# First batch: the sums of four values as products with a matrix of ones and zeros, taken from local windows that are loaded at the beginning

## The chip, the cores and the metric

The kernel runs on one core of a Trainium2 chip. The metric is device microseconds of that core for one execution. The core has TensorE (PE, with its weight loads shown as PEld), VectorE (DVE), ScalarE (ACT), GpSimd (POOL), and SyncE (SP), whose queue issues every DMA of this kernel. Each engine works through its own instructions in a fixed order; semaphores make one engine wait for another or for a DMA.

## The reference, cut to what matters

Attention for 4 batches of 8 heads, 576 positions of 64 numbers; each output is a coarse attention over means of four positions plus a local attention over a band of plus or minus three positions. Then a softplus MLP, then a mixture of experts with one expert per token.

```python
q_d = q.reshape(B, H, Sd, factor, D).mean(axis=3)      # factor = 4, Sd = 144
k_d = k.reshape(B, H, Sd, factor, D).mean(axis=3)
v_d = v.reshape(B, H, Sd, factor, D).mean(axis=3)      # the sums of four values
out_up = np.repeat(sm_attn(q_d, k_d, v_d), factor, axis=2)
mask = np.abs(pos[:, None] - pos[None, :]) < factor
scores = np.where(mask, scale * np.matmul(q, k.transpose(0, 1, 3, 2)), -1e9)
out_local = np.matmul(softmax(scores), v)
...
x = softplus(x @ w_in) @ w_out                         # 2304 x 512, 512 x 2048 x 512
out = gate * relu(x @ w1[e]) @ w2[e]
```

## The kernel before

Attention is cut into jobs. For each batch there are four `Down` jobs (one for each pair of heads, `hp`), which do the coarse attention, and twelve `Local` jobs (three thirds `j` of the positions, four pairs of heads). A job has six steps (`st_T`, `st_S`, `st_E`, `st_N`, `st_Ta`, `st_PV`): transposes, scores, exponentials, normalisation, transposes of the weights, products with the values. The steps of successive jobs are interleaved with lags of 0, 2, 3, 4, 6 and 7, and a scheduler puts the instructions of each engine into their final order.

**The head.** Before the MLP begins, the jobs of batch 0 run alone as far as its first 384 tokens need. In this part the first weights of the MLP are converted as well: `w_in` and `w_out` come as 64-bit floats, each chunk of 512 KB is loaded into a tile with the tag `raw` and turned into 32-bit floats by `from_f64`, one ACT instruction (L439) and four DVE instructions (L440 to L443). There are 32 chunks: four are converted in the head, the rest in the first block of the MLP (block 0), between its products `ph` (L579) and `py` (L619, L622) and the attention of batch 1.

**Tiles.** The tag `raw` has six buffers. They hold the weight chunks, the values `vr` of each `Down` job, and from batch 1 on its queries and keys `qr`, `kr`. For batch 0, `qr` and `kr` take other tags. The `Local` jobs read windows of 70 positions of the values: a tile `lv` (three buffers) holds three windows for four heads and is filled by three DMAs (L291). All these loads stand in SP's one queue, in program order as the scheduler leaves it, so that a load which waits for a free buffer holds back all loads behind it.

**The sums of four values.** A `Down` job loads its values as 72 partitions with rows of four positions (`vr`, L144), and `pre` adds them up: for batch 0 in one DVE reduction (L160), for later batches in three POOL additions (L155, L158). The result `vs` is an operand of `st_PV` (L248).

**Clock.** `warm` puts extra products with the identity matrix (L264) between the attention's products of the head.

In the tables and rows, `pT` and `pA` are transposes, `pS` scores, `pO` products with values, `dmx` the row maxima of a `Down` job, `de` its exponentials, `ls` those of a `Local` job, `laT` and `daT` the transposed weights, `xN` and `xf` the attention's output, `cva` the working tile of a conversion. A TensorE product of 32-bit floats leaves two records in the trace, so "x6" of them are three products.

Of the kernel before, what the change touches and what calls it, by code (L numbers as in the profile page):

```python
# [9 lines left out]
F32 = mybir.dt.float32  # L10
# [4 lines left out]
ALU = mybir.AluOpType  # L15
# [3 lines left out]
B, H, S, D = 4, 8, 576, 64  # L19
NT, DM, DFF = 2304, 512, 2048  # L20
E, FE = 8, 1024
FACTOR = 4
SD = S // FACTOR
SDH = SD // 2
# [5 lines left out]
TH = 192  # L30
NTH = S // TH
QB = 64
QD = SD // 3
KW = QB + 6
# [8 lines left out]
NC1 = DFF // 128  # L43
# [12 lines left out]
def band_attention__softplus_mlp__top1_moe(  # L56
# [14 lines left out]
    nc = tc.nc  # L71
# [49 lines left out]
    class Down:  # L121
# [3 lines left out]
        def load(self):  # L125
            b, h0 = self.b, 2 * self.hp
            self.raw = []
            for src, nm in ((q, "qr"), (k, "kr")):
                tag = {"qr": "wis", "kr": "wos"}[nm] if b == 0 else "raw"
                on_pe = b < PE_TRANSPOSED  # L130
                t = mlp.tile([RP, RT, 2, D] if on_pe else [128, NBLK, 32], F32, tag=tag, name=nm,
                             bufs=RAWB if tag == "raw" else 2)
                for h in range(2):
                    if on_pe:
                        nc.sync.dma_start(out=t[:, :, h, :], in_=src[b, h0 + h].rearrange("(p r) d -> p r d", r=RT))
                        continue
                    for c in range(2):
                        p0 = h * D + c * 32
                        nc.sync.dma_start(
                            out=t[p0:p0 + 32],  # L140
                            in_=src[b, h0 + h, :, c * 32:(c + 1) * 32].rearrange("(n t) d -> t n d", t=32))
                self.raw.append(t)
            t = mlp.tile([SDH, 2, 2, FACTOR, D], F32, tag="raw", name="vr", bufs=RAWB)
            nc.sync.dma_start(  # L144
                out=t.rearrange("p h a r d -> p (h a) (r d)"),
                in_=v[b, h0:h0 + 2].rearrange("h (a p r) d -> p (h a) (r d)", a=2, p=SDH, r=FACTOR),
            )
            self.raw.append(t)

        def pre(self):  # L150
            self.vs = apool.tile([SDH, 2, 2, D], F32, tag="vs", name="vs", bufs=4)
            x = self.raw[2].rearrange("p h a r d -> p (h a) r d")
            o = self.vs.rearrange("p a h d -> p h a d")
            if 4 <= self.b * NPAIR + self.hp < 16:
                G.tensor_tensor(out=x[:, :, 0:2], in0=x[:, :, 0:2], in1=x[:, :, 2:4], op=ALU.add)  # L155
                for h in range(2):
                    hs = slice(2 * h, 2 * h + 2)
                    G.tensor_tensor(out=o[:, h], in0=x[:, hs, 0], in1=x[:, hs, 1], op=ALU.add)  # L158
            else:
                V.tensor_reduce(out=o, in_=self.raw[2].rearrange("p h a r d -> p h a d r"), axis=AX.X, op=ALU.add)  # L160
# [65 lines left out]
                             accum_out=self.den[:, i, :])  # L226

        def st_N(self):
            den = self.den[:, :, 0]
            V.tensor_scalar(den, den, 1e-9, float(FACTOR), ALU.add, ALU.mult)  # L230
            V.reciprocal(den, den)
            (G if self.b * NPAIR + self.hp >= 4 else V).tensor_tensor(out=self.at, in0=self.at, in1=self.den.to_broadcast([2 * QD, 3, SD]), op=ALU.mult)
# [22 lines left out]
    qkT, vw = {}, {}  # L255
# [10 lines left out]
    def pa(name):  # L266

        if not started[0]:
            nps[0] += 1
            if nps[0] % 2:  # L270
                return psy.tile([128, 512], F32, tag="py", name=name)
        return psa.tile([128, 512], F32, tag="pa", name=name)
# [3 lines left out]
    def pairs(n):  # L276
# [2 lines left out]
            return [(h, i) for i in range(n) for h in range(2)]  # L279
        return [(h, i) for h in range(2) for i in range(n)]  # L280

    class Local:
        def __init__(self, b, j, hp):
            self.b, self.j, self.hp = b, j, hp
            self.w0 = [min(max(TH * j + QB * i - 3, 0), S - KW) for i in range(3)]

        def load_v(self):
            hs = slice(2 * self.hp, 2 * self.hp + 4)
            t = apool.tile([KW, 3, 4, D], F32, tag="lv", name="lv", bufs=3)
            for i in range(3):  # L290
                nc.sync.dma_start(  # L291
                    out=t[:, i], in_=v[self.b, hs, self.w0[i]:self.w0[i] + KW, :].rearrange("h p d -> p h d"))
            vw[self.b, self.j, self.hp // 2] = t

        def pre(self):
            pass
# [91 lines left out]
    def load_after(n):  # L388

        while loads and loads[0][0] <= n:  # L390
            loads.pop(0)[1]()
# [28 lines left out]
    def make_mask():  # L420
        G.memset(mask, 0.0)
        for hh in range(2):
            for sl, lo in ((slice(0, 1), -3), (slice(1, 4), 0), (slice(4, 5), 3)):
                m = mask[hh * QB:(hh + 1) * QB, sl, :]
                n = sl.stop - sl.start
                for sgn, base in ((1, -lo), (-1, lo + 6)):
                    G.affine_select(
                        out=m, in_=m, compare_op=ALU.is_ge, fill=MASKED, base=base,
                        pattern=[[0, n], [sgn, KW]], channel_multiplier=-sgn,
                    )  # L430
# [376 lines left out]
    if 0:  # L807
        ps = pa("pW")
        for i in range(0):
            T.matmul(ps[:, :128], ident, ident, start=True, stop=True)  # L810
    jobs[0].pre()
    make_mask()
    load_after(-1)
    for st in range(12 + LAG):
        attn_to(pre_end[st])
# [213 lines left out]
```

## Time and profile before

| | |
|---|---|
| median of 3 runs | 798.44 us (793.97 to 799.4) |
| the profiled execution | 798.25 us, its span 796.2 us |
| busy, share of the span | PE 95%, DVE 69%, POOL 59%, ACT 57% |
| granted TensorE clock, mean over the span | 0.977 |

The profiled execution's own time is 2.05 us more than its span. A busy PE is not PE at its peak, since products are pipelined and their ends are modelled. Shares over the whole span hide that the program has three parts with different limits: the head up to some 64 us, block 0 up to some 156 us, and the rest.

### The profile page before, as it was taken

To read this page: it belongs to the slowest core of one execution; us is meant where nothing else is said; L and a number is where in the kernel's file an instruction comes from. 1 tells how busy PE (TensorE), PEld (TensorE's weight loads), DVE (VectorE), ACT (ScalarE), POOL (GpSimd) and SP (SyncE) were. 2 spreads that over 40 slices of the span, in tenths; PEclk is the share of its full clock that TensorE was granted. 3 is DMA by queue.
4 is the path that set the end of the run, shared out by engine and by line. 5 is a ranking of instruction groups with operands and counts; after the bars stand their busy time and mean duration, and the time that the engine had idled before them with its cause. 6 is when DMAs were issued, how large, how long until landed. Compare 5 with 4: busy or idle time off the path is not lost.

```text
span 796.2 us, 13871 instructions
## 1 busy us (share of the span) xinstructions
PE 752.5 (95%) x4917; PEld 658.4 (83%) x4918; DVE 551.7 (69%) x1103; ACT 451.8 (57%) x1164; POOL 472.6 (59%) x451
## 2 busy tenths in 40 slices
PE   5886998899999999999999999999989999999994
PEld 4664655579799989899999999999977889899893
DVE  6979999967885787988654675556996385275221
ACT  5835566656566646666565656475646265355332
POOL 3435623757776666867566666666689366455541
PEclk9866999999999999999999999999999999999998
DMA  8849666415100251301000100080102022002002
GB/s 195 189 92 274 186 209 178 83 23 116 26 12 16 64 88 31 68 22 51 2 12 12 52 2 1 1 331 1 40 1 79 21 61 80 0 1 80 1 0 84
DMA packets 111448, 55.46 MB, mean 70 GB/s; under 512 B 89594, under 2 KB 102412, under 8 KB 111372
## 3 DMA queue, kind: packets, MB, share of 16 engines
q1 hardware_dynamic: 111371, 54.50, 25.7%
q8 instruction: 41, 0.67, 0.4%
q14 instruction: 36, 0.29, 0.1%
HBM read 45.05 MB, written 9.44 MB: 68 GB/s over the span
## 4 chain that ended last, share of the span: by engine, by line
PE 69%; DVE 17%; issue 4%; ACT 3%; DMA 3%; POOL 2%; SPq 1%; DVEq 0%; POOLq 0%; ACTq 0%
PE py L622 18%; PE ph L582 18%; PE py L913 12%; PE ph L764 9%; PE pO L344 2%; PE pS L311 2%; DVE cva L442 2%; PE ph L579 2%; PE pA L336 2%; DVE cva L440 1%; DVE g L604 1%; PE pS L210 1%; DVE cva L441 1%; DVE g L605 1%; DMA vr<-in_v_dram 1%
## 5 line engine op out<-in xcount | busy, mean ns | idle before, releaser
L622 PE MATMUL py<-g,wos 128*128 128x384 f32 x1056 | 209.8, 341 | 7.2 <-ACT wos L478 4.0
L622 PEld LDWEIGHTS py<-g,wos 128*128 128x128 f32 x1056 | 181.9, 188 | 14.1 <-ACT wos L478 5.2
L582 PE MATMUL ph<-xT,wis 128*128 128x384 f32 x960 | 184.3, 339 | 0.4 <-POOL wis L479 0.4
L582 PEld LDWEIGHTS ph<-xT,wis 128*128 128x128 f32 x960 | 166.3, 188 | 2.7 <-POOL wis L479 1.0
L479 POOL TENSOR_TENSOR wos<-wo,wos 128x512 fp32r<-128x512 f32 x88 | 124.0, 1410 | 40.5 <-ACT wos L478 37.3
L479 POOL TENSOR_TENSOR wis<-wi,wis 128x512 fp32r<-128x512 f32 x80 | 107.1, 1340 | 53.0 <-ACT wis L478 46.4
L588 ACT ACTIVATE ga<-ph 128x384 f32<-128x384 f32 x96 | 46.7, 486 | 72.3 <-PE ph L582 62.6
L603 DVE SCALAR_TENSOR_TENSOR ga<-ph,ga 128x384 f32<-128x384 f32 x88 | 48.4, 550 | 47.5 <-ACT ga L590 47.2
L769 DVE TENSOR_TENSOR u<-ph,u 128x384 f32<-128x384 f32 x60 | 33.2, 555 | 60.3 <-PE ph L764 60.1
L764 PE MATMUL ph<-xs,ws 128*128 128x384 f32 x378 | 73.6, 337 | 1.3 <-DVE u L769 0.9
L325 ACT ACTIVATE ls<-ls,lst 128x70 f32<-128x70 f32 x144 | 49.3, 344 | 43.9 <-DVE lst L319 38.6
L478 ACT CAST wos<-wo 128x512 fp32r<-128x512 f32 x88 | 54.2, 617 | 33.7 <-PE py L622 32.3
L764 PEld LDWEIGHTS ph<-xs,ws 128*128 128x128 f32 x378 | 67.0, 188 | 5.1 <-DVE u L769 1.3
L605 DVE TENSOR_TENSOR g<-ga,g 128x384 fp32r<-128x384 f32 x80 | 69.5, 868 | 1.6
L913 PE MATMUL py<-wos,gs 128*128 128x512 f32 x270 | 68.2, 394 | 0.3 <-ACT gs L773 0.3
L331 POOL TENSOR_TENSOR ls<-ls,lst 128x210 f32<-128x210 f32 x48 | 31.4, 656 | 54.7 <-DVE lst L330 36.8
L604 DVE CAST g<-ga 128x384 fp32r<-128x384 f32 x80 | 58.4, 730 | 4.5 <-PE py L622 0.9
L913 PEld LDWEIGHTS py<-wos,gs 128*128 128x128 f32 x270 | 50.1, 188 | 10.0 <-issue 0.6
L590 ACT ACTIVATE ga<-ga 128x384 f32<-128x384 f32 x96 | 50.3, 524 | 2.0
L589 ACT ACTIVATE ga<-ga 128x384 f32<-128x384 f32 x96 | 50.4, 525 | 0.5
L479 POOL TENSOR_TENSOR wos<-w2s,wos 128x512 fp32r<-128x512 f32 x24 | 33.2, 1388 | 27.5 <-ACT wos L478 27.5
L478 ACT CAST wis<-wi 128x512 fp32r<-128x512 f32 x80 | 48.9, 611 | 0.4 <-PE ph L582 0.4
(163 smaller groups left out, 1293.4 us busy)
## 6 DMA issues: line engine op xcount, KB each, us to landing
raw<-in_moe_w_in_dram SPq DMA_DIRECT2D x16, 512.0 KB
raw<-in_moe_w_out_dram SPq DMA_DIRECT2D x16, 512.0 KB
lv<-in_v_dram SPq DMA_DIRECT2D x72, 70.0 KB
vr<-in_v_dram SPq DMA_DIRECT2D x16, 288.0 KB
ydram<-y SPq DMA_DIRECT2D x12, 384.0 KB
yb<-ydram SPq DMA_DIRECT2D x12, 384.0 KB
out_dram<-ob SPq DMA_DIRECT2D x18, 256.0 KB
qr<-in_q_dram SPq DMA_DIRECT2D x48, 72.0 KB
```

Of the source, the lines that this page charges most:

```text
L325: A.activation(s[:, i, :], s[:, i, :], AF.Exp, bias=st[:, 0, i], accum_out=st[:, 1, i])
L478: A.copy(w[:, 0], src)
L479: G.tensor_tensor(out=w[:, 1], in0=src, in1=w[:, 0].bitcast(F32), op=ALU.subtract)
L582: T.matmul(ps[:, :TB], wt[:, w, cc, :], xT[n][:, x, cc, :], start=(i == 0), stop=(i == 3 * CC - 1))
L589: A.activation(a, a, AF.Exp, scale=-1.0)
L590: A.activation(a, a, AF.Ln, bias=1.0)
L603: V.scalar_tensor_tensor(a, ps[:, :TB], 0.0, a, ALU.max, ALU.add)
L604: (A.copy if n < 1 else V.tensor_copy)(g[:, 0, :], a)
L605: (G if n < 1 else V).tensor_tensor(out=g[:, 1, :], in0=a, in1=g[:, 0, :].bitcast(F32), op=ALU.subtract)
L622: T.matmul(yps[n][dc][:, :TB], w[:, a, dsl], g[:, b, :], start=(c == 0 and i == 0), stop=(c == NC1 - 1 and i == 2))
L764: T.matmul(ps[:, :TB], ops[:, w, a, cc, :], xop[p, x][:, l, cc, :], start=i == 0, stop=i == 5)
L913: T.matmul(yps[n][t], g[:, a, t * 128:(t + 1) * 128], w[:, b, :], start=first and c == q and i == 0, stop=last and c == q + NQ and i == 2)
```

## The change

For batch 0 the loads of `vr` and the DVE reductions are gone. All six window tiles of batch 0 are loaded by the `load` of the second and the fourth `Down` job, nine DMAs each, into parts of the tile `wo` that the converted `w_out` needs only later, and not into `lv`. In `st_N` of the first and the third `Down` job, `sums` computes `vs` for two pairs of heads: ten TensorE products of 70 x 72 (the matrix `sel`) by 70 x 256 (a window of four heads), accumulated in a PSUM bank `pV`, then one copy by ACT and one by DVE. `make_sel` builds the matrix on POOL with two memsets and six `affine_select`, in a part of the tile `wi` that is not yet in use. Batches 1 to 3 keep `vr` and `pre`.

```diff
@@ Down.load
+            if b == 0:
+                if self.hp % 2:
+                    for j in range(NTH):
+                        load_window(b, j, self.hp // 2, early[j * 2 + self.hp // 2])
+                return
             t = mlp.tile([SDH, 2, 2, FACTOR, D], F32, tag="raw", name="vr", bufs=RAWB)
...
+        def sums(self):
+            g = self.hp // 2
+            ps = pa("pV")
+            for a in range(2):
+                for i, w in enumerate(range(4 * a, 4 * a + 5)):
+                    x0 = 72 - (16 * w - SDH * a)
+                    o = 0 if w == 0 else 2 if w == 3 * NTH - 1 else 1
+                    T.matmul(ps[:SDH, a * 256:(a + 1) * 256], sel[:, o, x0:x0 + SDH],
+                             early[(w // 3) * 2 + g][:, w % 3, :, :].rearrange("p h d -> p (h d)"), start=i == 0, stop=i == 4)
+            for h in range(2):
+                t = jobs[2 * (self.hp + h)].vs = apool.tile([SDH, 2, 2, D], F32, tag="vs", name="vs", bufs=4)
+                (V.tensor_copy if h else A.copy)(
+                    t, ps[:SDH, :].rearrange("p (a h d) -> p a h d", a=2, h=4)[:, :, 2 * h:2 * h + 2, :])
+
         def pre(self):
+            if self.b == 0:
+                return
...
         def st_N(self):
+            if self.b == 0 and self.hp % 2 == 0:
+                self.sums()
...
+    early = [wo[:KW, 4 + 2 * i:6 + 2 * i, :].rearrange("p c f -> p (c f)")[:, :3 * 4 * D].rearrange(
+        "p (i h d) -> p i h d", i=3, h=4) for i in range(2 * NTH)]
+    sel = wi[:KW, NC1 - 1].rearrange("p c f -> p (c f)")[:, :3 * 152].rearrange("p (o x) -> p o x", o=3)
+
+    def make_sel():
+        G.memset(sel, 0.0)
+        G.memset(sel[:, :, 72:88], 1.0)
+        for o in range(3):
+            m = sel[:, o, 72:88]
+            G.affine_select(out=m, in_=m, compare_op=ALU.is_ge, fill=0.0, base=-3 * o, pattern=[[-FACTOR, 16]],
+                            channel_multiplier=1)
+            G.affine_select(out=m, in_=m, compare_op=ALU.is_ge, fill=0.0, base=FACTOR - 1 + 3 * o, pattern=[[FACTOR, 16]],
+                            channel_multiplier=-1)
+
+    def load_window(b, j, g, t):
+        for i in range(3):
+            w0 = min(max(TH * j + QB * i - 3, 0), S - KW)
+            nc.sync.dma_start(out=t[:, i], in_=v[b, 4 * g:4 * g + 4, w0:w0 + KW, :].rearrange("h p d -> p h d"))
+        vw[b, j, g] = t
...
         def load_v(self):
+            if self.b == 0:
+                return
+            load_window(self.b, self.j, self.hp // 2, apool.tile([KW, 3, 4, D], F32, tag="lv", name="lv", bufs=3))
...
-    jobs[0].pre()
     make_mask()
+    make_sel()
```

Line numbers shift: L172 becomes L193, L210 L231, L239 L262, L248 L271, L264 L287, L291 L322, L311 L351, L336 L376, L344 L384, L456 L496, L460 L500. In the order of instructions, `wo` as an operand in the head is a window of values and `wi` is `sel`.

On PE, early in the head, before: the third set of transposes follows the first local scores.

```order
L210 MATMUL pS<-dkT,dbd_101 96x144 x3
L172 MATMUL pT<-ident,kr 128x96 x6
L311 MATMUL pS<-qkT 64x70 x6
L172 MATMUL pT<-ident,qr 128x96 x6
L210 MATMUL pS<-dkT,dbd_102 96x144 x3
L172 MATMUL pT<-ident,kr 128x96 x6
```

The same place on PE with the change:

```order
L231 MATMUL pS<-dkT,dbd_101 96x144 x3
L193 MATMUL pT<-ident,kr 128x96 x6
L351 MATMUL pS<-qkT 64x70 x6
L162 MATMUL pV<-wo,wi 72x256 x10
L193 MATMUL pT<-ident,qr 128x96 x6
L231 MATMUL pS<-dkT,dbd_102 96x144 x3
L193 MATMUL pT<-ident,kr 128x96 x6
```

The first ten products of the sums now stand between the first local scores and the third set of transposes; all behind them waits for the nine windows that they read.

On PE, in the middle of the head, before: from the transposes of the second `Down` job to the scores of the fourth.

```order
L344 MATMUL pO<-laT,lv 64x64 x6
L264 MATMUL pO<-ident 128x128
L239 MATMUL pA<-ident,de 72x96 x3
L248 MATMUL pO<-daT,vs 64x144
L311 MATMUL pS<-qkT 64x70 x6
L264 MATMUL pS<-ident 128x128
L239 MATMUL pA<-ident,de 72x96 x3
L210 MATMUL pS<-dkT,dbd_102 96x144 x3
```

The same place on PE with the change:

```order
L384 MATMUL pO<-laT,wo 64x64 x6
L287 MATMUL pO<-ident 128x128
L262 MATMUL pA<-ident,de 72x96 x3
L162 MATMUL pV<-wo,wi 72x256 x10
L271 MATMUL pO<-daT,vs 64x144
L351 MATMUL pS<-qkT 64x70
L231 MATMUL pS<-dkT,dbd_102 96x144 x3
```

The second ten stand ahead of the scores of the fourth `Down` job, from which its maxima, exponentials and normalisation follow on DVE and ACT.

On SP, from the third chunk of `w_in` to the second chunk of `w_out` (the first that is converted after the head), before:

```order
L456 DMA raw<-in_moe_w_in_dram 128x4x256
L139 DMA qr<-in_q_dram 32x18x32 x4
L139 DMA kr<-in_k_dram 32x18x32 x4
L144 DMA vr<-in_v_dram 72x4x256
L291 DMA lv<-in_v_dram 70x4x64 x3
L139 DMA qr<-in_q_dram 32x18x32 x4
L139 DMA kr<-in_k_dram 32x18x32 x4
L291 DMA lv<-in_v_dram 70x4x64 x3
L144 DMA vr<-in_v_dram 72x4x256
L460 DMA raw<-in_moe_w_out_dram 128x1024
```

The same place on SP with the change:

```order
L496 DMA raw<-in_moe_w_in_dram 128x4x256
L322 DMA lv<-in_v_dram 70x4x64 x4
L542 DMA wg<-in_moe_w_gate_dram 128x4x8
L139 DMA qr<-in_q_dram 32x18x32 x4
L139 DMA kr<-in_k_dram 32x18x32 x4
L149 DMA vr<-in_v_dram 72x4x256
L543 DMA bias_b<-in_moe_modality_bias_dram 128x16
L139 DMA qr<-in_q_dram 32x18x32 x4
L139 DMA kr<-in_k_dram 32x18x32 x4
L149 DMA vr<-in_v_dram 72x4x256
L500 DMA raw<-in_moe_w_out_dram 128x1024
```

The two window loads among the queries and keys of batch 1, which waited for buffers of `lv`, are gone from there; the windows of batch 1 stand further ahead, where the three buffers are free. Behind block 0 the order of every engine is as before.

## Rows read from the trace of the kernel before

**Rows 1.** The page, span in 40 equal slices: busy tenths, granted clock.

```profile
PE   5886998899999999999999999999989999999994
DVE  6979999967885787988654675556996385275221

```

**Rows 2.** Busy us by stretch: head, block 0, rest; then clock, DMA share, GB/s.

```profile
0.00:64.00 64.00, 46.18 (x417) 37.27 (x418) 48.03 (x107) 35.69 (x130) 26.09 (x53) 0.83 0.74 172
64.00:156.00 92.00, 85.69 (x483) 53.27 (x484) 91.76 (x196) 55.20 (x162) 45.79 (x42) 0.95 0.68 185
156.00:796.00 640.00, 620.64 (x4019) 567.86 (x4017) 411.86 (x802) 360.96 (x873) 400.68 (x358) 1.00 0.15 43
```

**Rows 3.** The same view in the head; columns PE, PEld, DVE, ACT, POOL, clock.

```profile
10.00:22.00 12.00, 9.50 (x80) 7.94 (x80) 10.79 (x22) 9.19 (x33) 3.72 (x7) 1.00 1.01 232
22.00:26.00 4.00, 4.00 (x30) 3.57 (x29) 3.38 (x6) 3.42 (x15) 1.54 (x3) 0.57 1.08 288
...
36.00:40.00 4.00, 1.88 (x20) 1.30 (x17) 4.00 (x7) 0.78 (x2) 4.00 (x4) 0.89 0.85 198
40.00:52.00 12.00, 11.91 (x80) 9.07 (x80) 6.64 (x19) 4.20 (x17) 4.52 (x6) 0.50 0.36 75
...
56.00:66.00 10.00, 3.08 (x47) 2.30 (x44) 8.05 (x21) 4.07 (x17) 3.96 (x6) 0.68 0.95 256
```

**Rows 4.** The chain that ended last, 0 to 20 us: start, duration, what.

```profile
3.56 4.83 DMA vr<-in_v_dram
8.42 1.93 DVE vs L160
...
11.06 1.75 PE pS L210 x6
```

**Rows 5.** Groups of DVE instructions, 0 to 30 us.

```profile
L160 DVE TENSOR_REDUCE vs<-vr 72x256 f32<-72x1024 f32 x4 | 7.7, 1931 | 1.4 <-DMA vr<-in_v_dram 1.4
```

**Rows 6.** Groups of DVE instructions, 40 to 64 us.

```profile
L339 DVE COPY laT<-pA 70x384 f32<-70x384 f32 x3 | 1.6, 544 | 0.0
```

**Rows 7.** Groups of ACT instructions, 0 to 45 us.

```profile
L242 ACT COPY daT<-pA 72x288 f32<-72x288 f32 x8 | 3.1, 400 | 0.0
```

**Rows 8.** Groups of PE instructions, 80 to 126 us (granted clock 1.00).

```profile
L619 PE MATMUL py<-gN,wo 128*128 128x384 f32 x56 | 19.5, 489 | 0.0
...
L210 PE MATMUL pS<-dkT,dbd 128*96 128x144 f32 x18 | 2.7, 289 | 0.0
```

**Rows 9.** SP's queue in order of time, 40 to 60 us.

```profile
43.92 0.41 SPq L144 DMA_DIRECT2D vr<-in_v_dram  x1
49.24 1.27 SPq L291 DMA_DIRECT2D lv<-in_v_dram  x3
...
56.56 1.37 SPq L291 DMA_DIRECT2D lv<-in_v_dram  x3
58.03 0.36 SPq L144 DMA_DIRECT2D vr<-in_v_dram  x1
58.49 0.36 SPq L460 DMA_DIRECT2D raw<-in_moe_w_out_dram  x1
```

**Rows 10.** What SP's queue waited for, 0 to 140 us: total, times, longest.

```profile
SPq L291 <- PE pO L344: 6.6, 2, 4.8
```

**Rows 11.** The chain that ended last, 28 to 50 us.

```profile
38.29 1.66 DVE de L232
...
40.09 1.15 PE pA L239 x6
```

**Rows 12.** DVE in order of time, 58 to 68 us.

```profile
63.68 1.41 DVE L440 TENSOR_SCALAR cva<-cva 128x512 f32<-128x512 f32 x1 [1.95 <-ACT cva L439]
```

**Rows 13.** POOL in order of time, 0 to 14 us.

```profile
1.71 3.47 POOL L427 TENSOR_SCALAR_AFFINE_SELECT mask<-mask 64x70 f32<-64x70 f32 x12
11.77 0.67 POOL L185 TENSOR_TENSOR ds<-qkT 128x288 f32<-128x288 f32 x1 [6.59 <-DVE qkT L177]
```

More of the change, by code (lines that the diff above doesn't have):

```diff
@@ L287, in load_v @@
         def load_v(self):
[L288 to L293, printed above, removed]
+            if self.b == 0:
+                return
+            load_window(self.b, self.j, self.hp // 2, apool.tile([KW, 3, 4, D], F32, tag="lv", name="lv", bufs=3))
         def pre(self):
```

## The prediction

> **What bounds the kernel now.** I read the slices of the page first [rows 1]: PE is at nine tenths or more nearly everywhere except in the first four slices, and DVE is full in the stretch behind them. The table of busy times by stretch makes three parts of it [rows 2]. In the rest (156 to 796 us) PE is busy 620.6 of 640 us; the change touches nothing there. In block 0 (64 to 156 us) DVE is busy 91.8 of 92 us: the conversion of the weights sets the pace. In the head (0 to 64 us) no engine is full: PE 46.2, DVE 48.0, ACT 35.7 of 64 us. All that the change edits lies in the head, so the question is how much earlier or later block 0 can begin. A microsecond there is a microsecond at the end, since DVE in block 0 and PE behind it leave no slack. The second thing to read is the clock: the head as a whole is granted 0.83, and within it 40 to 52 us stands at 0.50, that is 1.2 instead of 2.4 GHz, with PE busy 11.91 of 12 us [rows 3]. Ahead of that stretch PE is busy only 1.88 of 4 us; in the chain, TensorE's next transposes at 40.09 us wait for the DVE normalisation `de` that ends at 39.95 [rows 11].
>
> The sum is made against the profiled execution, 798.25 us, which is 0.2 us under the median of the runs (798.44). Those runs spread from 794.0 to 799.4, and about 1% (8 us) is what a measurement of this kernel can tell from no change.
>
> **What goes.** DVE loses four reductions of 1.93 us, 7.7 us [rows 5]. The first is on the chain: DVE waits for `vr` until 8.42 us and the first scores start only at 11.06 [rows 4]. Without it that wait and 1.93 us go there. But what is late next are the nine windows, which the sums right behind the first scores need. They stand behind eight loads of queries and keys; I expect them to land near 13 us, about when PE reaches the first sums, so I count the 1.9 us at nothing and keep it as a bound on the good side. The other three reductions lie beside work of PE and ACT. SP loses four loads of 288 KB, and nine window loads move ahead, 630 KB; the DMA engines are busy throughout 10 to 22 us at 232 GB/s [rows 3], which makes 1152 KB about 5.0 us and 630 KB about 2.7 us. So the first weight chunks come about 2 us earlier at most; their conversion is placed behind attention steps, so this is worth nothing.
>
> **What comes: twenty products of 256 columns on PE.** No such product is in the trace. In block 0, 56 records of L619, that is 28 products of 384 columns, take 19.5 us, 0.70 us each, or 0.46 for 256 columns; nine products L210 of 144 columns take 2.7 us, 0.30 each, or 0.53 [rows 8]. The twenty cost 9.3 to 10.7 us at the full clock. I take 9.3, since 256 lies in a dense run of ten, like L619. At the half clock it would be twice that.
>
> The first ten (4.6 us) fall into 10 to 22 us, where PE is idle for 2.5 us [rows 3]; that much is absorbed, and 2.1 us is left. The second ten (4.6 us) fall behind 26 us, where PE works without a gap up to the idle time of 36 to 40 us, so they add in full: 6.8 us. There PE is idle for 2.1 us because `de` of the fourth `Down` job comes late out of a DVE queue full of conversions [rows 3, 11]. With PE 6.8 us later, its other products last until `de` is done; the gap closes: **+4.7 us** at the place that is 40 us now.
>
> **Small additions.** Four copies out of PSUM, two on DVE and two on ACT: the nearest rows are 0.54 us on DVE for 384 columns and 0.40 on ACT for 288 [rows 6, 7]. The two on DVE are under a seventh of what it loses; ACT, nearly full between 14 and 36 us, takes 0.8 us more, and I count that inside PE's delay. If that cover is gone it costs 0.8 us. POOL builds `sel` with two memsets and six selects right after the mask: the mask's twelve take 3.47 us, so six about 1.8, and POOL then stands idle for 6.59 us before its first sum at 11.77 [rows 13]; nobody waits. The windows sit in parts of `wo` and `wi` whose conversions come in block 0, long after the last reader: nothing.
>
> **The clock, term three.** If PE has no gap where it now waits from 38 to 40 us, the fall to 0.50 that follows has no occasion. At full speed the 11.9 us of products in 40 to 52 us would be 6.0. The other engines then limit: DVE has 6.64 us of work there [rows 3], so at most 5.4 us can come back. Steps of one job wait for each other across four engines, so I take 4.0: the balance becomes **+0.7 us**. Bounds: 0, if the clock stays as it is, and 6.0, with a further 1.7 us if the half-speed stretch at 22 to 26 us (granted 0.57) goes as well.
>
> **The queue, term four.** Block 0 cannot start its conversions before the second chunk of `w_out` is there. SP issues it at 58.49 us, behind a window load at 56.56 that had waited for a buffer of `lv` and another at 49.24 that had held the queue for 4.8 us [rows 9, 10]. DVE then stands idle for 1.95 us until 63.68 [rows 12]. With the change both window loads are gone from this place. The queries, keys and `vr` ahead of it still wait for `raw` buffers that DVE's transposes of batch 1 free, so the load moves by about the 2 us of window issue and not by more; DVE's idle time goes: **-2.0 us**, bounds 0 and 2.5.
>
> **Sum.** 798.25 + 4.7 - 4.0 - 2.0 = 796.95, so **797.0 us**. With no help from the clock it is 798.25 + 2.7 = 801.0. With both stretches at full speed and the 1.9 us at the start it is 798.25 + 4.7 - 6.0 - 1.7 - 1.9 - 2.0 = 791.3.
>
> **Rivals.**
> The clock stays as it is: 801.0. For it: PE was busy 11.91 of 12 us at 0.50 and was not given back its speed [rows 3], so filling PE is no warrant. Against it: the fall followed the gap that the change closes.
>
> Full speed through the whole head: 791.3. For it: twenty dense products in a part that had only short ones. This is what the Trainium skill would have, in "TensorE: Matmul & The Clock Gate", section "Part 1: The HAM clock gate (the "warmup" mystery)": the throttled state is the default, and sustained activity releases it. The 12 us at 0.50 with PE busy throughout speak against that rule as the page puts it, and the measurement decides; so it has a small chance.
>
> DVE and not PE bounds the head: then PE's products fill gaps, and block 0 begins earlier by what DVE loses, 7.7 less 1.1 for two copies, and by the 2.0 of its idle time: 798.25 - 6.6 - 2.0 = 789.6. For it: DVE has 10.79 of 12 us in 10 to 22. Against it: DVE has only 6.64 of 12 us in 40 to 52, where PE is full [rows 3].
>
> Slower than before: the sums themselves run at half the clock. The mechanism is the wait in front of them: PE stops at the first ten until nine windows have landed, and the row shows a half-speed stretch at 22 to 26 us behind a part with idle time. Each ten then costs 4.6 us more: 805.6 for one, 810.2 for both, with the rest of the clock as it is. It decides if the windows land later than some 15 us, so that PE has a gap like that of 36 to 40 us.
>
> The head's shift doesn't reach the end, because the pace of block 0 hides it: 798.3. Against it: DVE has 0.2 us of slack in 92 us there [rows 2].
>
> **How the numbers follow.** Forecast (797.0, own range 793 to 800) 0.40; clock as it is (801.0) 0.22; no effect at the end (798.3) 0.12; full clock (791.3) 0.10; DVE bounds (789.6) 0.10; sums at half the clock (over 805) 0.06. Faster by over 1% is below 790.5: most of the DVE case and an edge of the full clock, 0.10. Slower by over 1% is above 806.4: the last case, 0.07 with its edge. Within 1%: 0.83. The range leaves out the last case and half of the DVE case: 790 to 803.5.
>
> **What would show it.** The profile of the changed kernel should have 40 records of L162 in two runs of about 4.6 us each. The first run should start near 13 us with little idle time in front; a wait for a DMA there above 1 us makes the price of the start wrong. The reduction of batch 0 is gone from DVE. The clock in the stretch behind 40 us decides between 797 and 801. The second `w_out` chunk should be issued about 2 us earlier against the attention around it, and DVE's wait for ACT in front of that conversion should be gone; if it stays, term four is wrong. If block 0 begins earlier or later and the total does not follow, the reading of block 0 is wrong.

## The result, and the profile after

The changed kernel takes 800.28 us (median of 20 runs, 794.9 to 803.8), the kernel before 795.2 us on the same chip (20 runs, 791.1 to 800.3). The ratio is 1.0057, with an interval from 1.0039 to 1.0075: slower by 4.5 us (5.1 by the medians), where a gain of 1.3 us was forecast. The kernel before was also 3 us faster in these runs than in the profiled execution (798.25 us) that the sum was made against.

The busy times by stretch of the changed kernel answer to [rows 2] and [rows 3]. Columns are PE, PEld, DVE, ACT, POOL, then granted clock, share of the DMA engines, GB/s.

```profile
0.00:64.00 64.00, 53.62 (x460) 40.94 (x461) 40.79 (x102) 35.65 (x128) 28.41 (x62) 0.99 0.72 167
64.00:156.00 92.00, 84.11 (x477) 53.07 (x478) 90.70 (x198) 56.18 (x166) 42.04 (x39) 0.95 0.62 175
156.00:796.00 640.00, 622.56 (x4022) 570.04 (x4020) 406.53 (x803) 361.36 (x873) 401.82 (x358) 0.99 0.15 43
10.00:22.00 12.00, 12.00 (x45) 7.94 (x46) 3.49 (x10) 3.96 (x16) 1.63 (x3) 1.00 0.81 181
...
40.00:52.00 12.00, 11.77 (x140) 9.40 (x140) 11.36 (x29) 8.36 (x36) 6.61 (x8) 1.00 0.53 99
```

In the head PE has 7.4 us more and DVE 7.2 us less to do than before. The clock column rose from 0.83 to 0.99, and 40 to 52 us is at 1.00, where it was at 0.50. But DVE stands idle for 23.2 us of the head (64 less 40.79), before for 16.0 (64 less 48.03): the work that was taken off DVE became idle time. PE's timeline tells where. Columns are start, duration, instruction, and in brackets the idle time in front of it.

```profile
13.37 8.81 PE L162 MATMUL pV<-wo,wi 70*72 70x256 f32 x20
21.97 1.17 PE L193 MATMUL pT<-ident,qr 96*128 96x96 f32 x6
...
33.13 4.48 PE L162 MATMUL pV<-wo,wi 70*72 70x256 f32 x20
```

The same ten products (20 records) take 8.81 us the first time and 4.48 the second: 0.88 and 0.45 us each. The first ten ran at half speed, and so did the transposes behind them (1.17 us for six records; later in the same trace 0.66). The column of the granted clock shows 1.00 there all the same, so at the beginning of these traces the duration of a known product is the better clock. DVE's timeline has the other end of it, and its first conversion of block 0:

```profile
22.70 0.67 DVE L198 COPY qkT<-pT 128x288 f32<-128x288 f32 x1 [6.10 <-PE pT L193]
...
64.67 0.41 DVE L480 TENSOR_SCALAR cva<-cva 128x512 f32<-128x512 f32 x1
```

DVE waits 6.10 us for the transposes behind the first ten. At 64.67 it doesn't wait for ACT any more (1.95 us in [rows 12]), and SP issues the second `w_out` chunk at 56.61, 1.9 us earlier than in [rows 9]:

```profile
56.61 0.35 SPq L500 DMA_DIRECT2D raw<-in_moe_w_out_dram  x1
```

At the front of SP's queue it is the other way round. First the two first chunks of `w_in` before, then nine windows and these two chunks after:

```profile
18.04 0.97 SPq L456 DMA_DIRECT2D raw<-in_moe_w_in_dram  x2
```

```profile
6.35 4.39 SPq L322 DMA_DIRECT2D wo<-in_v_dram  x9
20.62 0.96 SPq L496 DMA_DIRECT2D raw<-in_moe_w_in_dram  x2
```

The chunks go out 2.6 us later. Nine window loads of 70 KB take 4.39 us of SP's time; each of the four `vr` loads of 288 KB that went took 0.58 to 0.91.

The earlier `w_out` chunk isn't worth anything at the end. A line's summary gives the duration (least, median, greatest, ns) and the first and last start. First the 64 products of block 0 (128 records) before, then after:

```profile
L579 PE MATMUL ph<-xN,wi x128: 485/486/847, 69.4 to 175.0; 128*128 128x384 f32 x128
```

```profile
L619 PE MATMUL ph<-xN,wi x128: 485/486/848, 66.9 to 176.5; 128*128 128x384 f32 x128
```

The first starts 2.5 us earlier, the last 1.5 us later. From the last one to the end of the span it is 621.2 us before and 621.3 after, so what this change costs arises ahead of the last product of block 0. (In the twenty profiles of this study that stretch takes 621.2 to 624.7 us; in some of the other kernels up to 3.5 us of the difference lie there.) Ahead of it DVE's conversions run nearly without a gap behind the head (90.70 of 92 us). Their last line, `wo`, in a second execution of the kernel before (before_again, below) and in the changed kernel:

```profile
L443 DVE SCALAR_TENSOR_TENSOR wo<-raw,cva x16: 657/681/1407, 39.7 to 151.1; 128x512 int32<-128x512 int32 x16
```

```profile
L483 DVE SCALAR_TENSOR_TENSOR wo<-raw,cva x16: 650/680/1080, 43.3 to 155.3; 128x512 int32<-128x512 int32 x16
```

The last conversion starts 4.2 us later, and the last product of block 0 4.3 us later (176.5 against 172.2 in before_again), though the first product starts at 66.9 us in both. In this pair what counts is how much of DVE's work is done when the head ends (50.33 us there, 7.7 of it reductions, 40.79 after), not when the first product starts. In the profile that the prediction rests on, the last conversion starts at 154.8 us: two executions of one kernel lie 3.7 us apart here, so a single profile settles no difference of that size.

### The profile page after: what moved, and what is told of

It is laid out like the page before. It is cut to its first block, busy times and chain, and to the rows that moved or that the text cites. A ratio compares the mean times of both kernels' runs of the same rounds, so it can differ in the third digit from the quotient of the medians.

```text
span 797.8 us, 13950 instructions
## 1 busy us (share of the span) xinstructions
PE 760.3 (95%) x4957; PEld 664.0 (83%) x4958; DVE 538.0 (67%) x1101; ACT 453.2 (57%) x1166; POOL 472.3 (59%) x459
## 4 chain that ended last, share of the span: by engine, by line
PE 72%; DVE 17%; ACT 4%; issue 3%; DMA 2%; POOL 1%; SPq 0%; DVEq 0%; ACTq 0%
PE py L662 19%; PE ph L622 17%; PE py L953 12%; PE ph L804 10%; DVE cva L482 2%; PE pO L384 2%; PE pS L351 2%; PE ph L619 2%; PE pA L376 2%; DVE cva L480 1%; DVE g L644 1%; PE pS L231 1%; DVE ga L643 1%; PE pV L162 1%; DVE g L645 1%
## 5 line engine op out<-in xcount | busy, mean ns | idle before, releaser
L409 POOL TENSOR_TENSOR xT<-xf,xT 128x192 fp32r<-128x192 f32 x40 | 31.0, 776 | 34.4 <-DVE xT L408 29.5
```

## The experiments

Theory A: the half speed of the first ten costs the time. Theory B: the amount of work on PE does. Rivals that came up with the first results: the early loads do (C), or the speed that TensorE is granted in the head, which depends on the gaps that each edit opens or closes (D). All ratios are against the kernel before, run beside it on the same chip.

| kernel | what is edited | us | ratio, interval |
|---|---|---|---|
| before_again | nothing | 795.1 | 1.0001, 0.9977 to 1.0026 |
| sums_later | after, first ten later | 799.3 | 1.0057, 1.0029 to 1.0085 |
| warm_after | after, 8 products at the start | 802.2 | 1.0090, 1.0054 to 1.0125 |
| warm_before | before, 8 products at the start | 805.9 | 1.0139, 1.0115 to 1.0164 |
| win_early | before, early loads | 800.8 | 1.0102, 1.0052 to 1.0151 |
| sums_few | after, 4 of 20 products | 798.0 | 1.0039, 1.0010 to 1.0068 |
| sums_none | after, no products | 800.7 | 1.0063, 1.0031 to 1.0095 |
| sums_twice | after, 40 products | 807.6 | 1.0161, 1.0112 to 1.0210 |
| none_late | before, no reductions | 808.6 | 1.0164, 1.0130 to 1.0199 |
| reduce_const | after's loads, DVE reduces | 801.5 | 1.0066, 1.0040 to 1.0092 |
| win_pool | after, loads by POOL | 816.5 | 1.0269, 1.0235 to 1.0302 |
| after_no_fill | after, no fillers | 804.6 | 1.0106, 1.0071 to 1.0141 |
| before_no_fill | before, no fillers | 797.8 | 1.0022, 0.9996 to 1.0048 |
| none_late_fill | none_late, 64 fillers | 795.2 | 0.9988, 0.9969 to 1.0006 |
| before_fill | before, 64 fillers | 802.2 | 1.0079, 1.0050 to 1.0109 |
| after_fill | after, 64 fillers | 809.5 | 1.0206, 1.0157 to 1.0256 |
| later_fill | sums_later, 64 fillers | 818.0 | 1.0295, 1.0255 to 1.0335 |
| none_early_fill | sums_none, 64 fillers | 803.7 | 1.0112, 1.0074 to 1.0150 |

**before_again.** No edit; the kernel before once more.

> The kernel before, unchanged, once more: a second execution of it with a trace, and a measure of what no change looks like. Both theories: ratio 1.000 within 0.003. The profile of before that the prediction rests on took 798.25 us, 3 us over the median of its 20 runs; if the half-speed stretch at 40 to 52 us belongs to that one execution, this trace lacks it, and the term of the prediction that gives 4.0 us back for it counted a loss that the usual execution doesn't have.

Measured 1.0001. Its profile (span 794.3 us) has the half-speed stretch again: 0.52 at 40 to 44 us and 0.50 at 44 to 48. The last product of block 0 starts at 172.2 us, 2.8 us earlier than in the profile of the prediction, so that one profile lay 2 to 3 us above the usual one.

**sums_later.** The first ten products are called one stage later.

```
         def st_N(self):
-            if self.b == 0 and self.hp % 2 == 0:
-                self.sums()
...
         def st_Ta(self):
+            if self.b == 0 and self.hp % 2 == 0:
+                self.sums()
```

> The changed kernel with the sums called in the step st_Ta and not in st_N, so that on TensorE the first ten products stand behind the third set of transposes and two sets of scores. Theory A (the clock): the first ten ran at half speed, 8.8 us where the second ten took 4.5, because TensorE had not yet been given its full speed; later they run at full speed, about 4.5 us, and the time falls by about 4 us, to 796 us, a ratio of 1.001 to before. Theory B (the amount): twenty products in a head that TensorE bounds cost the same wherever they stand; the time stays at 800 us, ratio 1.006.

The products ran as theory A wanted, in PE's timeline:

```profile
17.80 4.54 PE L162 MATMUL pV<-wo,wi 70*72 70x256 f32 x20
22.17 0.66 PE L262 MATMUL pA<-ident,de 96*72 96x96 f32 x6
```

The ten cost 4.54 in place of 8.81 us, and the time is the same as that of the changed kernel (1.0057 both). The windows show where the 4.3 us went:

```profile
28.00:32.00 4.00, 1.66 (x19) 1.32 (x19) 3.91 (x10) 3.94 (x14) 1.41 (x2) 0.85 0.50 86
32.00:36.00 4.00, 4.00 (x26) 3.42 (x25) 2.87 (x7) 2.11 (x9) 2.09 (x2) 0.50 0.85 159
```

PE, earlier by that much, has a gap (1.66 of 4 us), and half speed follows. Theory A falls for the total; that the gap took the 4.3 us back is a reading of these windows, not a test.

**warm_after and warm_before.** Eight products of the identity at the very beginning, to bring the speed sooner.

```
-    if 0:
+    if 1:
         ps = pa("pW")
-        for i in range(0):
+        for i in range(8):
             T.matmul(ps[:, :128], ident, ident, start=True, stop=True)
```

> The changed kernel with eight products of 128 columns with the identity matrix at the very beginning, while TensorE waits for the first loads (nothing reads their result). Theory A: if they raise the clock before the first ten products, those take about 4.5 us and the time falls to about 796 us; if the records show the first ten still at 8.8 us, the test says nothing on the time but that such products do not raise the clock. Theory B: 800 us or up to 2 us more, ratio 1.006 to 1.008.

> The kernel before with the same eight products at the beginning: the control of the run with them in the changed kernel. Both theories: within 2 us of before, ratio 0.998 to 1.003, since the head of before is not bound by its first scores.

Both are misses: slower by 7 and 11 us than the kernel before. In warm_after the first transposes took 0.66 to 0.69 us, full speed; then it was taken back, and the ten products ran at half speed again (8.74 us). Its windows:

```profile
8.00:12.00 4.00, 3.19 (x26) 2.68 (x25) 2.07 (x4) 1.94 (x6) 1.09 (x2) 0.59 0.78 175
12.00:24.00 12.00, 12.00 (x40) 8.29 (x39) 3.56 (x9) 4.40 (x17) 1.13 (x2) 0.50 0.79 180
```

Behind 12 us PE is busy without a gap and stays at 0.50 for 12 us. Why warm_before loses as much as 11 us its profile doesn't settle: that execution took 799.2 us, 7 less than the median of its runs.

**win_early.** The kernel before, with the first batch's windows loaded at the beginning; the reductions and their own loads stay.

```
+            if b == 0 and self.hp % 2:
+                for j in range(NTH):
+                    load_window(b, j, self.hp // 2, early[j * 2 + self.hp // 2])
```

> The kernel before with one part of the change: the first batch's local values are all loaded at the beginning into the unused chunks, while the sums stay reductions on VectorE with their own loads. Kernel before: median 795.2. If the products are what costs (too much TensorE work in the head, or the half speed of the first ten), this one keeps none of the loss: 793 with the queue's term of the prediction (2.0 us), 795 without it. If the loss of the changed kernel comes from the loads at the beginning or from the order that they bring, 798 to 800.

It loses 5.9 us by the medians without any sums on PE (8 by the ratio; one of its six runs took 811.2 us, the others 799.9 to 802.1). Nine more windows, 630 KB, stand at the beginning, and the `vr` loads that the changed kernel drops are still there: the first `w_in` chunk goes out at 26.02 us (18.04 before, 20.62 in the changed kernel), and DVE waits 4.2 us for `vr` (1.4 before). So its loss can be more than what the loads cost in the changed kernel.

**sums_few, sums_none, sums_twice.** The number of products, with the loads and the copies of the changed kernel. sums_few:

```
-                for i, w in enumerate(range(4 * a, 4 * a + 5)):
+                for i, w in enumerate(range(4 * a, 4 * a + 1)):
```

sums_none copies from `ident` in place of `ps` and has no products. sums_twice:

```
-            for a in range(2):
+            for a in (0, 1, 0, 1):
```

> The changed kernel with one product of the five per half, 4 of 20 in all; four fifths of each sum are left out. Changed kernel: median 800.3. Of 13.3 us of products (8.8 and 4.5) 10.6 go. If TensorE's work in the head is the price, microsecond for microsecond, 790; if half of it lies beside other work, 795; if the price is only the half speed of the first ten (7.0 us of their 8.8 go), 793 to 796; if the loss lies in the loads, in the copies of the sums or in the order, 799 to 801.

> The changed kernel without any product: the tiles of the sums are filled by the same two copies each from a constant, so the first batch's coarse values are left out. It tells what taking the reductions off VectorE was worth. If they stood on the path that sets the end, as the prediction says of the first of them (2.5 us) and of the queue behind them (2.0 us), 788 to 791; if their 7.7 us only become idle time of VectorE, 794 to 796, and the products alone then cost 4 to 6; if the loss lies in the loads, 799 to 801.

> The changed kernel with each ten products made twice (the second time over the first): 13 us more of TensorE work in the same two places, of which 9 us at half speed if the first twenty run as the first ten did, 4.5 us at full. If the amount sets the price, microsecond for microsecond, 810 to 814; if a price of 5 us for 13 us of products holds on, 805; if what the first ten cost is hidden by waits behind them, 800 to 802.

0, 4, 20 and 40 products give 800.7, 798.0, 800.3 and 807.6 us. The last twenty cost 7.3 us, the first twenty nothing that the intervals (about 3 us) can tell: theory B as a price by the microsecond falls too. Nor did the reductions' removal give anything, since sums_none has neither reductions nor products and is no faster. Its windows suggest why the products are free:

```profile
12.00:16.00 4.00, 2.40 (x24) 1.84 (x23) 2.21 (x7) 3.96 (x17) 0.00 (x0) 1.00 0.84 189
16.00:20.00 4.00, 4.00 (x34) 3.64 (x35) 2.10 (x6) 2.36 (x7) 1.63 (x3) 0.62 0.88 199
20.00:28.00 8.00, 7.14 (x44) 5.41 (x42) 3.49 (x10) 5.26 (x22) 2.88 (x5) 0.55 0.92 255
28.00:40.00 12.00, 10.51 (x73) 8.44 (x73) 6.18 (x17) 7.96 (x33) 4.45 (x4) 0.61 0.85 160
```

Without them PE has a gap at 12 to 16 us, and 24 us at little over half speed follow; DVE is idle for 24.3 us of the head. In sums_twice the first twenty products took 17.34 us, all at half speed, and the second twenty 8.80.

**none_late, reduce_const.** Loads and reductions one at a time. none_late is the kernel before without the first batch's reductions and `vr` loads; reduce_const is the changed kernel with the reductions back on DVE, over a constant, in place of `sums`. In none_late:

```
         def pre(self):
+            if self.b == 0:
+                return
```

In reduce_const:

```
+                x = ident[:SDH, :D].rearrange("p (o e d) -> p o e d", o=1, e=1).to_broadcast([SDH, 4, FACTOR, D])
+                V.tensor_reduce(out=self.vs.rearrange("p a h d -> p (a h) d"), in_=x.rearrange("p a r d -> p a d r"),
+                                axis=AX.X, op=ALU.add)
```

> The kernel before without the first batch's reductions and without their loads; the sums' tiles are filled from a constant by two copies each, as in sums_none, so the first batch's coarse values are left out. The local values are loaded as in the kernel before. sums_none (800.7) did the same with the early loads. If the early loads cost the 5 us, 788 to 794; if taking 7.7 us off VectorE only turns into idle time and the loads cost nothing, 794 to 797; if the head without the reductions is slower by itself (its order, or a TensorE that idles and then runs at half speed), 799 to 802.

> The changed kernel's loads with the reductions back on VectorE, over a constant of the same size (so the first batch's coarse values are left out, and no load of their own stands in the queue); no products. Kernel before 795. If the early loads cost the 5 us, 799 to 803; if the loads cost nothing and the head without reductions is slower by itself, 793 to 796.

reduce_const loses as much as the changed kernel with the reductions on DVE and nothing on PE (four of 1.21 us here, where those of the kernel before took 1.93). So from before to after in this order the loads cost 5.2 us, and the two other steps nothing: 1.0066, 1.0063 (sums_none), 1.0057 (after). But reduce_const is not a test of the loads alone: its head is granted 0.81 and its block 0 0.91 (before_again 0.87 and 0.94), with 0.50 throughout 44 to 64 us, so theory D's speed is a rival for these 5.2 us. In the other order it doesn't add up: none_late, with the loads left alone, was forecast at 788 to 802 and took 808.6. Its windows:

```profile
16.00:20.00 4.00, 2.09 (x21) 1.90 (x21) 3.12 (x9) 3.83 (x18) 1.91 (x4) 1.00 0.92 270
20.00:28.00 8.00, 7.12 (x40) 5.54 (x40) 6.14 (x14) 6.02 (x19) 3.43 (x6) 0.57 0.82 158
...
40.00:44.00 4.00, 1.66 (x14) 1.55 (x15) 1.94 (x6) 2.66 (x14) 2.73 (x4) 0.67 0.49 79
44.00:64.00 20.00, 20.00 (x129) 14.89 (x127) 5.96 (x18) 5.57 (x24) 1.82 (x4) 0.50 0.19 38
```

Two gaps of PE (2.09 and 1.66 of 4 us busy), half speed behind each, and in the second case 20 us with PE full at 0.50 and DVE busy only 5.96 of 20 us. Here PE at half speed is the bound of the head: SP waits 13.3 us for a product of PE (L356) that frees a buffer of `lv`, and the second `w_out` chunk goes out at 64.20 us.

**win_pool.** The early loads are issued by GpSimd's queue.

```
-            nc.sync.dma_start(
+            (nc.gpsimd if b == 0 else nc.sync).dma_start(
```

> The changed kernel with the 18 early loads issued by GpSimd's queue in place of SyncE's. SyncE's first loads of w_in then go out some 8.8 us earlier (two rows of nine loads of 4.39 us each stand before them). If the early loads cost by their place in SyncE's queue, 795 to 797; if by the bandwidth that they take from the others, 799 to 802; if the loss has nothing to do with the loads, 800 too, and the two are then told apart by none_late.

A miss, and not the test that it was meant to be: the loads stand on POOL between the mask and `sel`, the last three selects of `sel` start at 20.68 us, and PE stands for 7.17 us in front of the first product.

**after_no_fill, before_no_fill.** Both kernels have 20 filler products of the identity (`warm`, read by nobody); here they have none.

```
         if 4 <= nloc[0] < 12:
-            for i in range(1):
+            for i in range(0):
                 T.matmul(ps[:, 384:384 + 128], ident, ident[:, :128], start=True, stop=True)
```

> The changed kernel without its 20 filler products (identity by identity, nobody reads them; 9.26 us of TensorE's time between 31 and 57 us). There TensorE was busy nearly without a gap at full speed. If its work sets the head and the 20 sums alone hold its speed, 793 to 797; if gaps open without the fillers and half speed follows, 800 to 806, with a granted clock well under 0.99 in the first 64 us; if neither matters to the end, 800.

> The kernel before without its 20 filler products (11.3 us of TensorE's time, part of it at half speed). If the speed that is granted in the head sets its length, a lower clock than 0.83 there and 798 to 805; if TensorE's amount of work sets it, 788 to 793; if neither, 795.

Taking 9.3 us of work off a PE that was nearly full made the changed kernel 4.4 us slower. The windows show a gap and half speed behind it:

```profile
40.00:44.00 4.00, 1.62 (x16) 1.38 (x18) 3.97 (x14) 3.26 (x16) 1.93 (x4) 0.65 0.74 118
44.00:64.00 20.00, 17.87 (x158) 13.70 (x155) 17.16 (x43) 9.13 (x41) 9.19 (x15) 0.50 0.67 165
```

But these are not shown to be the cause. DVE did more in this head than in the changed kernel's (44.87 us, 40.79), and its last conversion starts at 153.6 us, not at 155.3. The loss comes later: the last product of block 0 starts at 177.5 us (176.5), and from there to the end it is 624.7 us (621.3). Why is open.

The kernel before loses 1.7 us by the ratio, 3.8 at most by its interval. That the shorter work and the longer half speed (0.50 from 40 to 60 us) about cancel there is a reading that no run tests.

**none_late_fill.** More fillers, from an earlier point on: 64 in place of 20, where the expectation says twice as many.

```
-        if 4 <= nloc[0] < 12:
-            for i in range(1):
+        if 2 <= nloc[0] < 12:
+            for i in range(2):
```

> none_late (808.6; granted clock 0.72 in the first 64 us, at half speed from 44 to 64 us with TensorE busy throughout) with fillers twice as many and from an earlier point on; the first batch's coarse values are left out there too. If the half speed is what made none_late slow and gaps before it are its cause, the clock stays up and the time falls to 794 to 802 in spite of more than 10 us of added products; if the amount of work sets the head, 812 to 820.

With 44 products more, that nobody reads, the kernel is 13.4 us faster than none_late. The same windows as of none_late:

```profile
16.00:20.00 4.00, 4.00 (x46) 3.81 (x45) 2.78 (x7) 3.27 (x15) 1.58 (x3) 1.00 0.97 280
20.00:28.00 8.00, 7.70 (x79) 6.58 (x77) 6.62 (x15) 6.96 (x26) 3.24 (x5) 1.00 0.75 157
...
40.00:44.00 4.00, 4.00 (x47) 3.30 (x46) 1.65 (x6) 1.79 (x8) 2.54 (x3) 1.00 0.53 116
44.00:64.00 20.00, 17.64 (x181) 14.09 (x180) 16.36 (x42) 9.17 (x40) 7.86 (x14) 0.84 0.71 168
```

No gap, no half speed up to 56 us, and SP issues the second `w_out` chunk at 50.91 us, 13.3 us earlier. This is the strongest evidence for D. It is not D alone: the fillers also change the order that the scheduler makes on DVE and SP.

**before_fill, after_fill, later_fill, none_early_fill.** The same edit in four other kernels.

> The kernel before with the fillers of none_late_fill (twice as many, from an earlier point on). If half speed in the head (0.50 at 40 to 48 us) costs it anything that fillers give back, 790 to 794; if the reductions on VectorE are then what it waits for, so that none_late_fill's 795.2 is the better for having none, 797 to 803; if the head's length does not reach the end, 795.

> The changed kernel with the same fillers. It was at full speed from 25 to 62 us already, with TensorE busy nearly all the time, so more fillers are only more work there: 803 to 812 if TensorE's work sets its head; 794 to 799 if half speed was still what cost it.

> sums_later (799.3; first ten products at full speed, then a gap at 29 us and half speed from 30 to 38 us) with the same fillers. If the gap and the half speed took back what the full speed of the first ten had given, 793 to 797; if the products' amount is the cost, 800 to 808.

> sums_none (800.7; no products, early loads, half speed from 16 to 40 us) with the same fillers; the first batch's coarse values are left out. Against none_late_fill (795.2) only the loads differ. If the early loads cost nothing by themselves, 794 to 797; if they cost what the changed kernel lost, 799 to 802.

With the speed held up everywhere (0.97 to 1.00 in these four heads, 0.95 in none_late_fill) the three parts of the change differ as follows, by the ratios times 795 us. Reductions and their loads gone: none_late_fill against before_fill, 7.2 us gained. Early loads: none_early_fill against none_late_fill, 9.9 us lost. Products: after_fill against none_early_fill, 7.5 us lost. By the medians it is 6.6, 8.2 and 5.8 us, so each is known to some 2 us. later_fill, with the products later, is worse still. The last conversions in before_fill, none_late_fill and none_early_fill tell which of these arise in the head:

```profile
L443 DVE SCALAR_TENSOR_TENSOR wo<-raw,cva x16: 671/679/1102, 36.7 to 149.6; 128x512 int32<-128x512 int32 x16
```

```profile
L455 DVE SCALAR_TENSOR_TENSOR wo<-raw,cva x16: 653/678/1078, 34.8 to 150.4; 128x512 int32<-128x512 int32 x16
```

```profile
L475 DVE SCALAR_TENSOR_TENSOR wo<-raw,cva x16: 653/678/1390, 36.5 to 155.5; 128x512 int32<-128x512 int32 x16
```

In these profiles the 7.2 us are not a price of the head. before_fill has its conversions done earlier than any other kernel here, and still the last product of block 0 starts at 178.0 us (171.6 in none_late_fill): PE waits 4.3 us for DVE's `ls` up to 147.7 us and is then busy without a gap. What the reductions cost is not shown by this pair.

The loads' price can be followed in part. In none_early_fill the first `w_in` chunk goes out at 20.64 us, in none_late_fill at 15.52; the first conversion on DVE starts 2.8 us later (26.23 against 23.45), the last 5.1, and the last product of block 0 7.7 (179.3 against 171.6). So 2.8 us are there early in the head, and the rest comes up behind it. The chain of waits of none_early_fill shows one place where the loads cost (start, duration, what):

```profile
30.71 0.47 SPq L149
31.18 0.04 issue
31.22 4.43 DMA lv<-in_v_dram
35.66 0.02 POOLq L511
35.68 1.66 POOL vr L168
37.34 1.68 POOL wis L511
39.02 0.83 POOL vs L171 x2
39.85 0.87 POOL ls L363
40.72 0.04 issue
40.76 0.52 PE pA L368 x3
```

SP's queue has been issuing without a pause since the windows; batch 1's `vr` goes out at 30.71 us, POOL's first sum over it starts at 35.68, and behind it in POOL's queue stands the softmax product `ls` that PE's transposes need. In none_late_fill that sum starts 2.5 us earlier:

```profile
33.14 1.71 POOL L165 TENSOR_TENSOR vr<-vr 72x512 f32<-72x512 f32 x1
```

No version beat the kernel before; none_late_fill equals it, and it leaves sums out.

## Why the prediction was wrong

Its time was missed by 3.3 us and the sign was wrong; against the kernel before it was missed by 5.8 us (1.3 less forecast, 4.5 more measured). By its own steps:

- **What goes.** The windows landed as forecast: the first ten started at 13.37 us with 0.2 us of waiting for a DMA. That the reductions' removal is worth nothing at the kernel's own number of fillers was right within some 3 us (sums_none against reduce_const). Wrong was to count the nine window loads moved ahead at nothing. **This is the step that failed.** The prediction priced them by their bytes, 2.7 us against 5.0 for the four `vr` loads, and had the first weight chunks come up to 2 us earlier. SP's queue spends its time by the load: the chunks went out 2.6 us later (20.62 against 18.04). win_early, the kernel before with the early loads, loses 5.9 us; with 64 fillers the loads cost 9.9. reduce_const loses 5.2 us with them, at a lower clock.
- **What comes.** The second ten took 4.48 us, forecast 4.6. The first ten took 8.81, because TensorE was still at half speed: 4.2 us mis-sized. At 10 to 22 us PE was busy 12.00 of 12 us. Put into the sum, this would give 801.2 us, close to the 800.3 measured. sums_later shows that the agreement is chance: with the first ten at 4.54 us the time didn't move.
- **The clock, term three.** In the profile it came about: the gap closed, and 40 to 52 us went from 0.50 to 1.00. As a gain on top of the rest it did not. sums_none shows that the kernel without products falls to half speed elsewhere; what the products cost and what they keep from being lost seem to be of the same size. (The term's bound of 6.0 us also goes beyond the 5.4 that the prediction itself allows there.)
- **The queue, term four.** The load moved by 1.9 us and DVE's 1.95 us of waiting went, as forecast. At the end nothing came: DVE had by then stood idle 7.2 us longer in the head.
- **"A microsecond there is a microsecond at the end."** Right from the last product of block 0 on (621.2 and 621.3 us to the end). Wrong for the beginning of block 0, on which terms three and four were read: its first product came 2.5 us earlier and its last 1.5 us later.
- **The rivals.** "Sums run at half the clock" was right in its price (4.2 us, forecast 4.6) and wrong in its mechanism, a wait for the windows: there was none, the speed had simply not come yet. "DVE bounds" (789.6) is refuted: its 7.2 us became idle time. The rule in the Trainium skill, "TensorE: Matmul & The Clock Gate", section "Part 1: The HAM clock gate (the "warmup" mystery)", that sustained activity releases the throttled state, does not describe these heads by itself: 17.34 us of dense products at half speed in sums_twice, and PE 20.00 of 20 us busy at 0.50 in none_late. In none_late_fill a TensorE without gaps kept its speed up to 56 us, which agrees with the rule.

Shown is that a loss of this size is there with the early loads and without any products (win_early, reduce_const, none_early_fill), that the products cost nothing net at the kernel's own number of fillers, within some 3 us, and that fillers, with the gaps and the speed that they change, move the time of one kernel by 13 us. The cause stays open in part: the early loads cost 5 to 10 us in three comparisons and spared 8 in the fourth (sums_none against none_late). The chain shows 2.5 us of the cost in POOL's queue, the conversions 2.8 us early in the head. The half speed in none_late can account for the fourth comparison's sign. But no run separates the loads from the order that the scheduler then makes, or from the speed that this order is granted.

## What to carry to other kernels

In a stretch where no engine is full, don't add up terms against one profile: work taken off one engine opens gaps on another, and where TensorE's gaps are followed by half speed, removing work can cost more than the work (here 13.4 us less for 44 useless products more). Read the price of a head from the engine that must finish behind it, by its idle time there, and check that this engine still ends last (in before_fill it didn't). Cost a load that is moved ahead by the time that its queue spends on it and by everything that is queued behind it, not by its bytes alone. Before a sum is called explained because its repaired terms agree, make the repair alone on the chip.

## What the runs showed of the hardware

- TensorE starts at half speed, and the profile's clock column doesn't show it: six records of the transposes take 1.17 to 1.21 us at the beginning and 0.66 later, under the same 1.00. In the profile of the kernel before the speed came between 14.60 us (1.01 us for six) and 17.10 (0.66), in before_again between 17.65 (1.17) and 20.18 (0.66), in the changed kernel only behind 22 us, though PE was busy 12.00 of 12 us.
- Behind eight products at the start the first transposes were at full speed in warm_after (0.66 us at 5.39 us), the second ones in warm_before (1.17 at 5.38, 0.72 at 6.92). It was taken back within 12 us (1.73 us for six scores at 11.84 in warm_before, 0.59 granted at 8 to 12 in warm_after); the kernel before became 11 us slower by them in the median.
- An f32 product of 256 columns with 70 rows takes 0.45 us at full and 0.87 to 0.88 us at half speed.
- SP's queue takes 4.39 us for nine loads of 70 KB (630 KB), and 0.58 to 0.91 us for one load of 288 KB.
